# A linear-attention and maxout kernel: PSUM tiles of one bank, output in token order, loads given out sooner

## The chip, the cores and the metric

The kernel runs on one core of a Trainium2 chip. The core has a matrix engine (TensorE, PE in the profile), three engines for elementwise work (VectorE or DVE, ScalarE or ACT, GpSimd or POOL) and SyncE (SP), which gives out most transfers. Each engine runs its own instructions in program order and waits on semaphores for the others. Matrix products land in PSUM, a memory of eight banks of 2 KB for each of 128 partitions; everything else lies in SBUF. The metric is device time in microseconds, and less is better.

## The reference

The first part is a linear attention with a decaying state, for 4 batches and 8 heads, 768 tokens and a head dimension of 48. The second is a layer with two weight matrices, the elementwise maximum of both products, and an output matrix.

```python
for t in range(S):
    kt, vt, rt, wt = k[:, :, t], v[:, :, t], r[:, :, t], w[:, :, t]
    cur = np.einsum('bhd,bhe->bhde', u[None] * kt, vt)
    y[:, :, t] = np.einsum('bhd,bhde->bhe', rt, state + cur)
    state = wt[:, :, :, None] * state + np.einsum('bhd,bhe->bhde', kt, vt)
# ...
x = y.transpose(0, 2, 1, 3).reshape(B * S, H * D)      # 3072 x 384
g = np.maximum(x @ w1, x @ w2)                          # d_ff = 1024
out = g @ w_out                                         # 3072 x 384
```

## The kernel before

The tokens are cut into 12 units of 256 tokens of one batch (three chunks of time, four batches each). Within a unit a row of 128 partitions holds two neighbouring tokens each (index i, even and odd), and the lower and the upper 64 partitions are the two halves of the unit (index b). The maximum is computed as relu(x (w1 - w2)) + x w2, so wd is w1 - w2, and wc is w2 @ w_out, formed once at the start.

The kernel is written as small operations, one for each step and unit, and a string ORDER lists them. Every engine runs its operations in that order. A tile that comes from a pool with so many buffers may only be given out again when the last user of the old one is done; the waits follow from that. The names that matter, for a unit n:

- w, k, r, v: loads. lw: ScalarE takes the logarithm of w. lp: GpSimd adds the two tokens of a row. cs: TensorE makes running sums. m, z: VectorE puts the exponents together. AO, AE, iA: ScalarE exponentials. rp, kp: VectorE scales r and k with them. rk, rku, dg, vd: the token's own term (GpSimd, GpSimd, VectorE, GpSimd). vb: GpSimd casts v.
- tr: TensorE transposes the scaled r and k. ev0, ev1: ScalarE and VectorE copy the transposes to SBUF.
- kv, Sa, S1, Tf, dec, S0, row, WL, Wt: the state and its decay.
- sc0, sc1: scores of the even and the odd tokens. M0, M1: VectorE masks them. yb, yi, ya: the three parts of y, summed in PSUM. xT: ScalarE copies y to SBUF.
- g0 to g3, r0 to r3: gates (TensorE) and relu (ScalarE). oc, oa, ob: the output matrix in three parts, for each half b. os: ScalarE copies the output to SBUF. out: the store.
- wd, wt, wcm, wce: weights at the start.

A stretch of ORDER for the middle of the kernel, and the start of it:

```
w.0 lw.0 k.0 r.0 u w2 rk.0 rku.0 dg.0 lp.0 cs.0 m.0 z.0 AO.0 AE.0 rp.0 iA.0 kp.0 v.0 vb.0 w.1 w1
wd.0 k.1 r.1 lw.1 kv.0 Sa.0 Tf.0 S1.0 tr.0 ev0.0 ev1.0 wd.1 wo lp.1 cs.1 m.1 z.1 AO.1 AE.1 vd.0
...
M0.5 AO.6 AE.6 rp.6 g3.4 r3.4 oc0.4 oa0.4 sc1.5 M1.5 iA.6 kp.6 rk.6
rku.6 dg.6 v.6 w.7 lw.7 k.7 r.7 vb.6 ob0.4 oc1.4 oa1.4 os0.4 out0.4 row.5 WL.5 dec.3 S0.3 ya.5
xT.5 tr.6 ev0.6 ev1.6 ob1.4 os1.4 out1.4 g0.5 r0.5 kv.6 Sa.6 S1.6 Tf.6 Wt.4 lp.7 cs.7 m.7 z.7
g1.5 g2.5 r1.5 r2.5 vd.6 yb.6 yi.6 sc0.6 M0.6 AO.7 AE.7 rp.7 g3.5 r3.5 oc0.5 oa0.5 sc1.6 M1.6
```

The parts of the code that the change touches, with cuts:

```python
LB = 3
ldp = tc.alloc_tile_pool(name="ld", bufs=LB)             # loads
def load(n, name, src):
    U[n][name] = t = ldp.tile([P, H, 2, D], F32, tag="l" + name, name="l" + name)
    nc.sync.dma_start(out=..., in_=...)                   # 384 KB
# ...
def tr(n):                                                # "sc": one buffer of two banks
    U[n]["tr"] = tp = pt_([P, 2, 2, 2, NP, Q], BF16, "sc")
    # ... 32 transposes into tp[:, b, j, i, p, :]
def evict(n, b, copy):
    U[n]["T", b] = t = wt_([P, 2, 2, NP, Q], BF16, f"T{b}")
    copy(t..., U[n]["tr"][:, b]...)
# ...
def scores(n, i):
    U[n]["sc", i] = sc = pt_([P, 2, NP, P], F32, "sc")
    # ... 16 matmuls into sc[q, e, p, :]
def masked(n, i):
    U[n]["M", i] = t = wt_([P, 2, NP, P], BF16, f"M{i}")
    nc.vector.tensor_mul(t..., U[n]["sc", i]..., mask[:, i]...)   # 1024 elements
# ...
def xT(n):
    U[n]["xT"] = t = wt_([P, 2, KO, P], BF16, "xT", 3)
    nc.scalar.copy(t.rearrange("c b k t -> c b (k t)"), U[n]["y"][:, :, 0:HD])
def gate(n, j):                                           # "go": two buffers of one bank
    U[n]["g", j] = g = pt_([P, 2, 2, P], F32, "go", 2)
    # ... 6 matmuls
def out_s(n, b):                                          # five buffers
    U[n]["s", b] = t = wt_([P, HD], F32, "osb", 5)
    nc.scalar.copy(t, U[n]["o", b])
def out_d(n, b):
    for i in range(2):                                    # even tokens, odd tokens
        nc.sync.dma_start(out=out[tok + i:tok + P:2, :],
                          in_=U[n]["s", b][i * Q:(i + 1) * Q, :])
```

The eight PSUM banks: two for the sums (ex), two for y and kv (y), two for transposes and scores (sc), two for gates and outputs (go).

Of the kernel before, what the change touches and what calls it, by code (L numbers as in the profile page):

```python
# [22 lines left out]
wce.2 k.2 r.2 rp.2 v.2 w.3 lw.3 vb.2 k.3 r.3 ya.1 g3.0 oc0.0 oa0.0 r3.0 xT.1 iA.2 kp.2 rk.2
rku.2 dg.2 row.1 WL.1 ob0.0 oc1.0 oa1.0 os0.0 ob1.0 os1.0 out1.0 g0.1 r0.1 out0.0 kv.2 Sa.2 S1.2
Tf.2 tr.2 ev0.2 ev1.2 g1.1 g2.1 r1.1 r2.1 lp.3 cs.3 m.3 z.3 vd.2 yb.2 yi.2 sc0.2 M0.2 AO.3 AE.3
rp.3 g3.1 oc0.1 oa0.1 r3.1 sc1.2 M1.2 ob0.1 oc1.1 oa1.1 v.3 w.4 vb.3 lw.4 k.4 r.4 iA.3 kp.3
os0.1 out0.1 ya.2 xT.2 rk.3 rku.3 dg.3 row.2 WL.2 tr.3 ev0.3 ev1.3 Wt.1 ob1.1 os1.1 out1.1 g0.2
r0.2 kv.3 Sa.3 S1.3 Tf.3 lp.4 cs.4 m.4 z.4 g1.2 g2.2 r1.2 r2.2 dec.0 S0.0 vd.3 yb.3 yi.3 sc0.3
M0.3 AO.4 AE.4 rp.4 g3.2 r3.2 oc0.2 oa0.2 dec.1 S0.1 sc1.3 M1.3 iA.4 kp.4 v.4 w.5 k.5 r.5 lw.5
row.3 WL.3 ob0.2 oc1.2 oa1.2 os0.2 out0.2 ya.3 xT.3 rk.4 rku.4 dg.4 tr.4 ev0.4 ev1.4 ob1.2 os1.2  # L30
out1.2 g0.3 r0.3 vb.4 kv.4 Sa.4 S1.4 Tf.4 lp.5 cs.5 m.5 z.5 g1.3 r1.3 g2.3 r2.3 vd.4 yb.4 yi.4
sc0.4 M0.4 Wt.2 dec.2 S0.2 AO.5 AE.5 rp.5 g3.3 r3.3 oc0.3 oa0.3 sc1.4 M1.4 iA.5 kp.5 v.5 w.6 k.6
r.6 lw.6 vb.5 rk.5 rku.5 dg.5 ob0.3 oc1.3 oa1.3 os0.3 out0.3 ya.4 xT.4 Wt.3 row.4 WL.4 tr.5
ev0.5 ev1.5 ob1.3 os1.3 out1.3 g0.4 r0.4 kv.5 Sa.5 S1.5 Tf.5 lp.6 cs.6 m.6 z.6 g1.4 r1.4 g2.4
r2.4 vd.5 yb.5 yi.5 sc0.5 M0.5 AO.6 AE.6 rp.6 g3.4 r3.4 oc0.4 oa0.4 sc1.5 M1.5 iA.6 kp.6 rk.6
rku.6 dg.6 v.6 w.7 lw.7 k.7 r.7 vb.6 ob0.4 oc1.4 oa1.4 os0.4 out0.4 row.5 WL.5 dec.3 S0.3 ya.5
xT.5 tr.6 ev0.6 ev1.6 ob1.4 os1.4 out1.4 g0.5 r0.5 kv.6 Sa.6 S1.6 Tf.6 Wt.4 lp.7 cs.7 m.7 z.7
g1.5 g2.5 r1.5 r2.5 vd.6 yb.6 yi.6 sc0.6 M0.6 AO.7 AE.7 rp.7 g3.5 r3.5 oc0.5 oa0.5 sc1.6 M1.6
iA.7 kp.7 dec.4 S0.4 Wt.5 rk.7 rku.7 dg.7 v.7 vb.7 w.8 lw.8 k.8 r.8 row.6 WL.6 dec.5 S0.5 ob0.5
oc1.5 oa1.5 os0.5 out0.5 ya.6 xT.6 tr.7 ev0.7 ev1.7 ob1.5 os1.5 out1.5 g0.6 r0.6 kv.7 Sa.7 S1.7  # L40
Tf.7 lp.8 cs.8 m.8 z.8 g1.6 r1.6 g2.6 r2.6 vd.7 yb.7 yi.7 sc0.7 M0.7 AO.8 AE.8 rp.8 g3.6 r3.6
oc0.6 oa0.6 sc1.7 M1.7 iA.8 kp.8 v.8 w.9 vb.8 lw.9 k.9 r.9 rk.8 rku.8 dg.8 ob0.6 oc1.6 oa1.6
os0.6 out0.6 ya.7 xT.7 row.7 WL.7 tr.8 ev0.8 ev1.8 ob1.6 os1.6 out1.6 g0.7 r0.7 kv.8 Sa.8 S1.8
lp.9 cs.9 m.9 z.9 g1.7 g2.7 r1.7 r2.7 vd.8 yb.8 yi.8 sc0.8 M0.8 AO.9 AE.9 rp.9 g3.7 r3.7 oc0.7
oa0.7 sc1.8 M1.8 iA.9 kp.9 rk.9 rku.9 dg.9 v.9 w.10 k.10 r.10 lw.10 vb.9 Wt.6 dec.6 S0.6 ob0.7
oc1.7 oa1.7 os0.7 out0.7 ya.8 xT.8 tr.9 ev0.9 ev1.9 ob1.7 os1.7 out1.7 g0.8 r0.8 kv.9 Sa.9 S1.9
lp.10 cs.10 m.10 z.10 g1.8 r1.8 g2.8 r2.8 vd.9 yb.9 yi.9 sc0.9 M0.9 AO.10 AE.10 rp.10 g3.8 r3.8
oc0.8 oa0.8 sc1.9 M1.9 iA.10 kp.10 v.10 vb.10 w.11 lw.11 ob0.8 oc1.8 os0.8 out0.8 oa1.8 ya.9
xT.9 rk.10 rku.10 dg.10 tr.10 ev0.10 ev1.10 k.11 r.11 ob1.8 os1.8 out1.8 g0.9 r0.9 kv.10 Sa.10
S1.10 lp.11 cs.11 m.11 z.11 g1.9 r1.9 g2.9 r2.9 vd.10 yb.10 yi.10 sc0.10 M0.10 AO.11 AE.11 rp.11  # L50
g3.9 r3.9 oc0.9 oa0.9 sc1.10 M1.10 iA.11 kp.11 rk.11 rku.11 dg.11 v.11 vb.11 ob0.9 oc1.9 oa1.9
os0.9 out0.9 Wt.7 dec.7 S0.7 ya.10 xT.10 ob1.9 os1.9 out1.9 g0.10 r0.10 tr.11 ev0.11 ev1.11
kv.11 Sa.11 S1.11 g1.10 r1.10 g2.10 r2.10 vd.11 yb.11 yi.11 sc0.11 M0.11 g3.10 r3.10 oc0.10
oa0.10 sc1.11 M1.11 ob0.10 oc1.10 oa1.10 os0.10 out0.10 ya.11 xT.11 ob1.10 os1.10 out1.10 g0.11
r0.11 g1.11 r1.11 g2.11 r2.11 g3.11 r3.11 oc0.11 oa0.11 ob0.11 oc1.11 oa1.11 os0.11 out0.11
ob1.11 os1.11 out1.11
"""


# [19 lines left out]
def _body(tc, r, k, v, w, u_in, moe_w1, moe_w2, moe_w_out, out):  # L79
    nc = tc.nc  # L80
    B, H, S, D = r.shape
    P = 128
# [246 lines left out]

    def evict(n, b, copy):  # L330
        U[n]["T", b] = t = wt_([P, 2, 2, NP, Q], BF16, f"T{b}")
        copy(t.rearrange("d j i p q -> d (j i p q)"),  # L332
             U[n]["tr"][:, b].rearrange("d j i p q -> d (j i p q)"))
# [123 lines left out]
    @op  # L459
    def xT(n):  # L460
        U[n]["xT"] = t = wt_([P, 2, KO, P], BF16, "xT", 3)
        nc.scalar.copy(t.rearrange("c b k t -> c b (k t)"), U[n]["y"][:, :, 0:HD])  # L462
# [38 lines left out]
    def out_d(n, b):  # L501
        c, bb = unit(n)
        tok = bb * S + c * C + b * P
        for i in range(2):
            nc.sync.dma_start(out=out[tok + i:tok + P:2, :],  # L505
                              in_=U[n]["s", b][i * Q:(i + 1) * Q, :])
# [45 lines left out]
```

## Time and profile before

| | |
|---|---|
| time | 171.19 us, median of 3 (169.57 to 171.47) |
| span of the profiled execution | 170.9 us |
| TensorE matmul busy | 136.6 us, 80% of the span |
| VectorE, ScalarE, GpSimd busy | 98.6, 94.1 and 96.0 us |
| moved by DMA | 28.19 MB, 165 GB/s in the mean |
| loads of w, k, r, v | 12 each of 384 KB |
| stores | 48 of 96 KB |

A line of groups names the line of the kernel, the engine, the operation and the tiles, then how many, the busy time and the mean of one in ns, then the idle time of the engine just before and what ended it. A line of a timeline begins with the start and the duration in us; what ended the idle time before it stands in brackets. In the slices each digit is a fortieth of the span, in tenths of busy time. A line of waits names the engine that waited, what it waited for, and the total, the number and the longest of the waits. "SPq" is the time in which SyncE gives out a transfer. TensorE's matmuls are pipelined, so the duration of one holds more than its share of the engine.

### The profile page before, as it was taken

To read this page: it belongs to the slowest core of one execution; us is meant where nothing else is said; L and a number is where in the kernel's file an instruction comes from. 1 tells how busy PE (TensorE), PEld (TensorE's weight loads), DVE (VectorE), ACT (ScalarE), POOL (GpSimd) and SP (SyncE) were. 2 spreads that over 40 slices of the span, in tenths; PEclk is the share of its full clock that TensorE was granted. 3 is DMA by queue.
4 is the path that set the end of the run, shared out by engine and by line. 5 is a ranking of instruction groups with operands and counts; after the bars stand their busy time and mean duration, and the time that the engine had idled before them with its cause. 6 is when DMAs were issued, how large, how long until landed. Compare 5 with 4: busy or idle time off the path is not lost.

```text
span 170.9 us, 6596 instructions
## 1 busy us (share of the span) xinstructions
PE 136.6 (80%) x2920; PEld 90.0 (53%) x2920; DVE 98.6 (58%) x144; ACT 94.1 (55%) x165; POOL 96.0 (56%) x91
## 2 busy tenths in 40 slices
PE   0003273999999599999799995997989999989990
...
PEclk9999997599999879999999999999999999999999
...
GB/s 141 234 235 404 258 231 210 72 232 323 22 72 239 194 69 300 114 113 301 73 221 207 51 196 199 153 274 88 188 235 105 176 50 263 112 50 6 92 15 81
DMA packets 63182, 28.19 MB, mean 165 GB/s; under 512 B 58153, under 2 KB 62377, under 8 KB 63153
## 3 DMA queue, kind: packets, MB, share of 16 engines
...
q8 instruction: 23, 0.38, 0.9%
...
## 4 chain that ended last, share of the span: by engine, by line
PE 30%; DMA 26%; ACT 12%; POOL 9%; DVE 8%; SPq 7%; issue 5%; ACTq 0%; POOLq 0%; DVEq 0%
DMA lw<-in_w_dram 15%; PE go L470 8%; PE go L494 7%; DMA u_b<-in_u_dram 4%; SPq L505 4%; PE go L217 3%; PE go L489 3%; POOL rku L302 3%; ACT T L332 3%; SPq L179 3%; DMA lv<-in_v_dram 3%; ACT xT L462 3%; DMA lk<-in_k_dram 3%; PE ex L237 2%; POOL rku L297 2%
## 5 line engine op out<-in xcount | busy, mean ns | idle before, releaser
L470 PE MATMUL go<-xT,wd_sb 128*128 128x256 bf16 x288 | 37.9, 276 | 3.4 <-ACT xT L462 3.2
L494 PE MATMUL go<-wo_sb,gT 128*128 128x384 bf16 x192 | 39.2, 331 | 0.0
L397 DVE TENSOR_TENSOR M<-sc,mask 128x1024 bf16<-128x1024 f32 x24 | 29.4, 1223 | 13.7 <-PE sc L393 13.7
L470 PEld LDWEIGHTS <-wd_sb 128*128 128x128 bf16 x288 | 27.3, 99 | 13.1 <-issue 7.1
L478 ACT ACTIVATE gT<-go 128x512 bf16<-128x512 f32 x48 | 28.7, 601 | 9.9 <-PE go L470 8.3
L297 POOL TENSOR_TENSOR rku<-lr,lk 128x768 f32<-128x768 f32 x12 | 21.8, 1817 | 8.2 <-DMA lr<-in_r_dram 8.2
L292 POOL CAST vn<-lv 128x768 bf16<-128x768 f32 x12 | 9.9, 826 | 26.9 <-DMA lv<-in_v_dram 20.1
L237 PE MATMUL ex<-lp,triS 128*128 128x384 f32 x24 | 12.3, 599 | 14.2 <-POOL lp L233 14.2
L302 POOL TENSOR_TENSOR rku<-rku,u_b 128x768 f32<-128x768 f32 x12 | 21.8, 1814 | 3.1 <-DMA u_b<-in_u_dram 2.3
L494 PEld LDWEIGHTS <-gT 128*128 128x128 bf16 x192 | 17.3, 98 | 11.5 <-issue 0.3
L313 POOL TENSOR_TENSOR vd<-lv,dg 128x768 bf16<-128x768 f32 x12 | 19.6, 1633 | 4.5 <-DVE dg L308 4.3
L308 DVE TENSOR_REDUCE dg<-rku 128x16 f32<-128x768 f32 x12 | 11.4, 949 | 16.8 <-POOL rku L302 16.8
L228 ACT ACTIVATE lw<-lw 128x768 f32<-128x768 f32 x12 | 10.1, 840 | 15.2 <-DMA lw<-in_w_dram 15.2
L332 DVE COPY T<-sc 128x1024 bf16<-128x1024 bf16 x12 | 8.3, 689 | 13.4 <-ACT T L332 13.3
L489 PE MATMUL go<-wc_sb,xT 128*128 128x384 bf16 x72 | 15.6, 326 | 0.0
L255 ACT ACTIVATE ex<-mz 128x384 f32<-128x384 f32 x12 | 5.9, 490 | 17.2 <-DVE mz L251 17.2
L233 POOL TENSOR_TENSOR lp<-lw 128x384 f32<-128x384 f32 x12 | 12.0, 998 | 6.0 <-ACT lw L228 5.9
L263 ACT ACTIVATE ex<-mz 128x768 f32<-128x768 f32 x12 | 9.8, 816 | 8.8 <-DVE rn L267 8.8
L499 ACT COPY osb<-go 128x384 f32<-128x384 f32 x24 | 11.5, 480 | 5.6 <-PE go L494 5.6
L271 DVE TENSOR_TENSOR kn<-lk,ex 128x768 bf16<-128x768 f32 x12 | 11.4, 946 | 5.3 <-ACT ex L263 5.3
L267 DVE TENSOR_TENSOR rn<-lr,ex 128x768 bf16<-128x768 f32 x12 | 11.4, 948 | 2.2 <-ACT ex L259 1.7
L332 ACT COPY T<-sc 128x1024 bf16<-128x1024 bf16 x12 | 12.2, 1017 | 0.7 <-PE sc L325 0.6
...
## 6 DMA issues: line engine op xcount, KB each, us to landing
...
out_dram<-osb SPq DMA_DIRECT2D x48, 96.0 KB, 2.3
...
```

What stands on the lines that cost most here:

```text
L233: nc.gpsimd.tensor_add(t, U[n]["lw"][:, :, 0, :], U[n]["lw"][:, :, 1, :])
L237: nc.tensor.matmul(EX[:, 0, 0:HD], triS, U[n]["lp"].rearrange("p h d -> p (h d)"))
L297: nc.gpsimd.tensor_mul(t, U[n]["r"], U[n]["k"])
L302: nc.gpsimd.tensor_mul(t, t, u_b.rearrange("p (h d) -> p h d", h=H).unsqueeze(1).to_broadcast([P, 2, H, D]))
L313: nc.gpsimd.tensor_mul(t.rearrange("p i h d -> p h i d"), U[n]["v"], U[n]["dg"].to_broadcast([P, H, 2, D]))
L332: copy(t.rearrange("d j i p q -> d (j i p q)"), U[n]["tr"][:, b].rearrange("d j i p q -> d (j i p q)"))
L397: nc.vector.tensor_mul(t.rearrange("s e p t -> s (e p) t"), U[n]["sc", i].rearrange("s e p t -> s (e p) t"), mask[:, i].rearrange("s i q - ...
L470: nc.tensor.matmul(g[:, f, :], wd_sb[:, ko, fo * P:(fo + 1) * P], U[n]["xT"][:, :, ko, :], start=(f == 0 and ko == 0), stop=(f == 1 and ko ...
L478: nc.scalar.activation(U[n]["gT"][:, 2 * j:2 * j + 2].rearrange("p f j t -> p (f j t)"), U[n]["g", j].rearrange("p f j t -> p (f j t)"), A ...
L489: nc.tensor.matmul(t, U[n]["xT"][:, b, ko, :], wc_sb[:, ko, :], start=(ko == 0), stop=False)
L494: nc.tensor.matmul(U[n]["o", b], U[n]["gT"][:, fo, b, :], wo_sb[:, fo, :], start=False, stop=(fo == FO - 1))
L499: nc.scalar.copy(t, U[n]["o", b])
```

## The change

Five things change together. The PSUM tiles for transposes and scores become two buffers of one bank each, in place of one buffer of two banks; a transpose tile is now one half b, a score tile one parity e of the heads, and the mask is applied in two instructions (Ma, Mb). xT writes the tokens in their order, so that an output half is 128 neighbouring tokens and one store writes it. The load buffers become four. And ORDER is written anew: loads stand further ahead of their use, the stores later, and TensorE works on the gates and outputs of one unit between the steps of the next, in another order than before.

The two banks are for letting TensorE refill one while the other is still read; the single store is for fewer issues on SyncE; the loads and buffers are for keeping the loads from standing behind the stores.

```diff
-w.0 lw.0 k.0 r.0 u w2 rk.0 rku.0 dg.0 lp.0 cs.0 m.0 z.0 AO.0 AE.0 rp.0 iA.0 kp.0 v.0 vb.0 w.1 w1
-wd.0 k.1 r.1 lw.1 kv.0 Sa.0 Tf.0 S1.0 tr.0 ev0.0 ev1.0 wd.1 wo lp.1 cs.1 m.1 z.1 AO.1 AE.1 vd.0
 ... (cut)
+w.0 k.0 r.0 u w2 rk.0 lw.0 lp.0 cs.0 m.0 z.0 rku.0 dg.0 AO.0 AE.0 rp.0 v.0 vb.0 w.1 w1 wd.2 k.1
+lw.1 r.1 iA.0 kp.0 tr.0 ev1.0 ev0.0 kv.0 Sa.0 S1.0 Tf.0 wd.0 lp.1 cs.1 m.1 z.1 row.0 wo vd.0
+yb.0 yi.0 sc1.0 M1a.0 M1b.0 AO.1 AE.1 rp.1 iA.1 rk.1 rku.1 v.1 vb.1 w.2 wt.0 lw.2 lp.2 sc0.0
+M0a.0 WL.0 wcm.0 dg.1 M0b.0 ya.0 xT.0 wd.1 wt.1 wcm.1 wt.2 vd.1 wce.0 kp.1 tr.1 cs.2 ev1.1 kv.1
 ... (cut)
+dg.5 vd.5 rk.6 rku.6 out1.0 g0.3 g1.3 r0.3 r1.3 g2.3 r2.3 g3.3 r3.3 rp.5 iA.5 row.4 WL.4 sc0.4
+oc0.3 oa0.3 ob0.3 os0.3 out0.3 v.6 w.7 vb.6 k.7 r.7 M0a.4 M0b.4 ya.4 xT.4 kp.5 tr.5 ev0.5 ev1.5
+cs.6 m.6 z.6 kv.5 Sa.5 S1.5 AO.6 AE.6 Tf.5 oc1.3 oa1.3 ob1.3 os1.3 out1.3 Wt.4 dec.4 S0.4 Wt.2
+dec.2 S0.2 yb.5 yi.5 sc1.5 M1a.5 M1b.5 g0.4 r0.4 g1.4 r1.4 g2.4 r2.4 g3.4 r3.4 row.5 WL.5 rp.6
+iA.6 sc0.5 out1.2 oc0.4 oa0.4 lw.7 lp.7 row.6 ob0.4 os0.4 oc1.4 Wt.3 WL.6 dec.3 S0.3 dg.6 vd.6
 ... (cut)
-    LB = 3
+    LB = 4
 ... (cut)
-        U[n]["tr"] = tp = pt_([P, 2, 2, 2, NP, Q], BF16, "sc")
+        U[n]["tr"] = tp = [pt_([P, 2, 2, NP, Q], BF16, "sc", 2) for b in range(2)]
-                            tp[:, b, j, i, p, :],
+                            tp[b][:, j, i, p, :],
-             U[n]["tr"][:, b].rearrange("d j i p q -> d (j i p q)"))
+             U[n]["tr"][b].rearrange("d j i p q -> d (j i p q)"))
 ... (cut)
-        U[n]["sc", i] = sc = pt_([P, 2, NP, P], F32, "sc")
+        U[n]["sc", i] = sc = [pt_([P, NP, P], F32, "sc", 2) for e in range(2)]
-                    nc.tensor.matmul(sc[q, e, p, :], t[d, 1, i, p, :], t[d, 0, :, p, :])
+                    nc.tensor.matmul(sc[e][q, p, :], t[d, 1, i, p, :], t[d, 0, :, p, :])
 ... (cut)
-    def masked(n, i):
-        U[n]["M", i] = t = wt_([P, 2, NP, P], BF16, f"M{i}")
+    def masked(n, i, e):
+        if e == 0:
+            U[n]["M", i] = wt_([P, 2, NP, P], BF16, f"M{i}")
         nc.vector.tensor_mul(
-            t.rearrange("s e p t -> s (e p) t"),
-            U[n]["sc", i].rearrange("s e p t -> s (e p) t"),
-            mask[:, i].rearrange("s i q -> s (i q)").unsqueeze(1).to_broadcast([P, H, P]))
+            U[n]["M", i][:, e], U[n]["sc", i][e],
+            mask[:, i].rearrange("s i q -> s (i q)").unsqueeze(1).to_broadcast([P, NP, P]))
 ... (cut)
-        nc.scalar.copy(t.rearrange("c b k t -> c b (k t)"), U[n]["y"][:, :, 0:HD])
+        nc.scalar.copy(t.rearrange("c b k (q i) -> c (b k) i q", i=2),
+                       U[n]["y"][:, :, 0:HD].rearrange("c b (k i q) -> c b k i q", k=KO, i=2))
 ... (cut)
-        for i in range(2):
-            nc.sync.dma_start(out=out[tok + i:tok + P:2, :],
-                              in_=U[n]["s", b][i * Q:(i + 1) * Q, :])
+        nc.sync.dma_start(out=out[tok:tok + P, :], in_=U[n]["s", b])
```

More of the change, by code (lines that the diff above doesn't have):

```diff
@@ L17 @@
 ORDER = """
-w.0 lw.0 k.0 r.0 u w2 rk.0 rku.0 dg.0 lp.0 cs.0 m.0 z.0 AO.0 AE.0 rp.0 iA.0 kp.0 v.0 vb.0 w.1 w1
-wd.0 k.1 r.1 lw.1 kv.0 Sa.0 Tf.0 S1.0 tr.0 ev0.0 ev1.0 wd.1 wo lp.1 cs.1 m.1 z.1 AO.1 AE.1 vd.0
-yb.0 yi.0 sc0.0 M0.0 sc1.0 rp.1 M1.0 iA.1 kp.1 rk.1 rku.1 dg.1 wd.2 ya.0 xT.0 tr.1 ev0.1 ev1.1
-v.1 vb.1 w.2 wt.0 wt.1 wcm.0 lw.2 wce.0 kv.1 Sa.1 S1.1 Tf.1 wcm.1 wce.1 g0.0 r0.0 vd.1 yb.1 yi.1
-sc0.1 M0.1 g1.0 g2.0 r1.0 r2.0 sc1.1 M1.1 row.0 WL.0 Wt.0 lp.2 cs.2 m.2 z.2 AO.2 AE.2 wt.2 wcm.2
@@ L23 @@
[L23 to L56, printed above, removed]
+w.0 k.0 r.0 u w2 rk.0 lw.0 lp.0 cs.0 m.0 z.0 rku.0 dg.0 AO.0 AE.0 rp.0 v.0 vb.0 w.1 w1 wd.2 k.1
+lw.1 r.1 iA.0 kp.0 tr.0 ev1.0 ev0.0 kv.0 Sa.0 S1.0 Tf.0 wd.0 lp.1 cs.1 m.1 z.1 row.0 wo vd.0
+yb.0 yi.0 sc1.0 M1a.0 M1b.0 AO.1 AE.1 rp.1 iA.1 rk.1 rku.1 v.1 vb.1 w.2 wt.0 lw.2 lp.2 sc0.0
@@ new lines @@
+M0a.0 WL.0 wcm.0 dg.1 M0b.0 ya.0 xT.0 wd.1 wt.1 wcm.1 wt.2 vd.1 wce.0 kp.1 tr.1 cs.2 ev1.1 kv.1
+m.2 ev0.1 Sa.1 Tf.1 S1.1 z.2 AO.2 AE.2 wce.1 wcm.2 wce.2 yb.1 yi.1 sc1.1 M1a.1 M1b.1 g0.0 r0.0
+g1.0 r1.0 g2.0 g3.0 r2.0 r3.0 k.2 r.2 rk.2 rku.2 rp.2 iA.2 dg.2 v.2 vb.2 vd.2 w.3 lw.3 lp.3 k.3
+r.3 rk.3 rku.3 v.3 w.4 k.4 r.4 vb.3 sc0.1 oc0.0 oa0.0 ob0.0 os0.0 oc1.0 out0.0 M0a.1 M0b.1 ya.1
+xT.1 Wt.0 dec.0 S0.0 kp.2 tr.2 ev1.2 cs.3 ev0.2 kv.2 Sa.2 S1.2 Tf.2 oa1.0 ob1.0 os1.0 row.1 m.3
+WL.1 z.3 AO.3 AE.3 yb.2 yi.2 sc1.2 M1a.2 M1b.2 g0.1 g1.1 r0.1 r1.1 g2.1 g3.1 r2.1 r3.1 row.2
@@ new lines @@
+WL.2 sc0.2 oc0.1 oa0.1 rp.3 iA.3 lw.4 lp.4 v.4 w.5 vb.4 k.5 r.5 v.5 w.6 k.6 r.6 ob0.1 oc1.1
+os0.1 out0.1 dg.3 vd.3 rk.4 rku.4 M0a.2 M0b.2 ya.2 xT.2 vb.5 kp.3 tr.3 ev1.3 ev0.3 cs.4 m.4 kv.3
+Sa.3 S1.3 Tf.3 Wt.1 dec.1 S0.1 oa1.1 ob1.1 os1.1 out1.1 z.4 AO.4 AE.4 yb.3 yi.3 sc1.3 g0.2 g1.2
+r0.2 r1.2 g2.2 r2.2 g3.2 r3.2 M1a.3 M1b.3 sc0.3 rp.4 iA.4 lw.5 lp.5 oc0.2 oa0.2 ob0.2 oc1.2
+os0.2 out0.2 dg.4 vd.4 rk.5 rku.5 lw.6 lp.6 M0a.3 M0b.3 ya.3 xT.3 kp.4 tr.4 ev1.4 ev0.4 cs.5
+kv.4 Sa.4 S1.4 Tf.4 row.3 WL.3 m.5 oa1.2 ob1.2 os1.2 z.5 AO.5 AE.5 yb.4 yi.4 sc1.4 M1a.4 M1b.4
@@ new lines @@
+dg.5 vd.5 rk.6 rku.6 out1.0 g0.3 g1.3 r0.3 r1.3 g2.3 r2.3 g3.3 r3.3 rp.5 iA.5 row.4 WL.4 sc0.4
[3 more added lines that the diff above has]
+iA.6 sc0.5 out1.2 oc0.4 oa0.4 lw.7 lp.7 row.6 ob0.4 os0.4 oc1.4 Wt.3 WL.6 dec.3 S0.3 dg.6 vd.6
+rk.7 rku.7 M0a.5 M0b.5 ya.5 xT.5 kp.6 tr.6 ev1.6 ev0.6 cs.7 m.7 kv.6 Sa.6 S1.6 Tf.6 oa1.4 ob1.4
@@ new lines @@
+os1.4 z.7 AO.7 AE.7 yb.6 yi.6 sc1.6 M1a.6 M1b.6 g0.5 g1.5 r0.5 r1.5 g2.5 r2.5 g3.5 r3.5 rp.7
+iA.7 dg.7 sc0.6 v.7 w.8 k.8 r.8 vb.7 lw.8 lp.8 vd.7 v.8 w.9 vb.8 rk.8 rku.8 oc0.5 oa0.5 ob0.5
+os0.5 oc1.5 out0.5 M0a.6 M0b.6 ya.6 xT.6 kp.7 tr.7 ev0.7 ev1.7 cs.8 m.8 kv.7 Sa.7 S1.7 Tf.7
+out0.4 Wt.6 dec.6 S0.6 oa1.5 ob1.5 os1.5 z.8 AO.8 AE.8 yb.7 yi.7 sc1.7 M1a.7 M1b.7 g0.6 g1.6
+r0.6 r1.6 g2.6 r2.6 g3.6 r3.6 rp.8 iA.8 out1.4 dg.8 vd.8 sc0.7 lw.9 lp.9 oc0.6 oa0.6 ob0.6 os0.6
+M0a.7 M0b.7 ya.7 xT.7 oc1.6 k.9 r.9 rk.9 rku.9 v.9 w.10 k.10 r.10 vb.9 lw.10 lp.10 kp.8 tr.8
@@ new lines @@
+ev1.8 ev0.8 cs.9 kv.8 Sa.8 S1.8 oa1.6 ob1.6 os1.6 row.7 WL.7 m.9 z.9 AO.9 AE.9 Wt.5 dec.5 S0.5
+out0.6 dg.9 vd.9 rk.10 rku.10 yb.8 yi.8 sc1.8 g0.7 g1.7 r0.7 r1.7 g2.7 r2.7 g3.7 r3.7 M1a.8
+M1b.8 sc0.8 rp.9 iA.9 oc0.7 oa0.7 ob0.7 os0.7 oc1.7 M0a.8 M0b.8 ya.8 xT.8 kp.9 tr.9 ev1.9 ev0.9
+cs.10 m.10 kv.9 Sa.9 S1.9 oa1.7 ob1.7 os1.7 yb.9 yi.9 sc1.9 z.10 AO.10 AE.10 g0.8 g1.8 r0.8 r1.8
+g2.8 r2.8 g3.8 r3.8 M1a.9 M1b.9 sc0.9 oc0.8 oa0.8 ob0.8 oc1.8 rp.10 iA.10 v.10 w.11 vb.10 lw.11
+lp.11 k.11 r.11 v.11 dg.10 vd.10 rk.11 rku.11 Wt.7 dec.7 S0.7 out1.5 os0.8 M0a.9 M0b.9 ya.9 xT.9
@@ new lines @@
+kp.10 tr.10 ev1.10 ev0.10 cs.11 m.11 kv.10 Sa.10 S1.10 z.11 AO.11 oa1.8 ob1.8 os1.8 yb.10 yi.10
+sc1.10 M1a.10 M1b.10 AE.11 dg.11 vd.11 g0.9 r0.9 g1.9 r1.9 g2.9 r2.9 g3.9 r3.9 rp.11 iA.11
+sc0.10 oc0.9 oa0.9 ob0.9 M0a.10 M0b.10 ya.10 xT.10 out1.7 kp.11 tr.11 ev0.11 ev1.11 out0.7 oc1.9
+vb.11 kv.11 Sa.11 S1.11 oa1.9 ob1.9 out0.8 yb.11 yi.11 sc1.11 M1a.11 M1b.11 out1.6 os0.9 os1.9
+out1.9 g0.10 r0.10 g1.10 r1.10 g2.10 r2.10 g3.10 r3.10 out0.9 sc0.11 oc0.10 oa0.10 ob0.10 os0.10
+oc1.10 out0.10 out1.8 M0a.11 M0b.11 ya.11 xT.11 oa1.10 ob1.10 os1.10 g0.11 r0.11 g1.11 r1.11
@@ L57 @@
+g2.11 r2.11 g3.11 r3.11 oc0.11 oa0.11 ob0.11 os0.11 out0.11 out1.10 oc1.11 oa1.11 ob1.11 os1.11
+out1.11
 """
```

3 lines of the change are left out of this document (2 added, 1 removed).

## The prediction

> **What bounds the kernel now.** I read the page's engine shares and slices first, to see which engine could set the end and where it stands idle.
>
> ```profile
> PE 136.6 (80%) x2920; PEld 90.0 (53%) x2920; DVE 98.6 (58%) x144; ACT 94.1 (55%) x165; POOL 96.0 (56%) x91
> PE   0003273999999599999799995997989999989990
> PEclk9999997599999879999999999999999999999999
> ```
>
> TensorE is full from slice 7 on, with notches; no other engine passes 60%. The kernel has three parts: a start of 35 us with little TensorE work, a middle in which TensorE is nearly the bound, and a tail. Busy TensorE time by stretch (the view of windows) gives the notches a size: in the nine stretches of 11 us from 46 to 145 us it is busy 10.47, 9.56, 11.00, 10.12, 11.00, 9.21, 9.98, 10.48 and 10.81 us, together 92.63 of 99. So 6.4 us are idle there. A unit without an idle gap takes about 10.5 us: the transposed output copy (xT) of two late units starts at 127.23 and 137.95, 10.7 us apart, less 0.19 us of waiting.
>
> Next the waits and the chain, to see what makes the notches. The first two lines are SyncE's own waits over the span and ScalarE's from 46 to 145 us (total, times, longest); the third is the page's chain by line.
>
> ```profile
> SPq L505 <- ACT osb L499: 36.9, 12, 6.6
> ACT lw L228 <- DMA lw<-in_w_dram: 13.1, 7, 3.0
> DMA lw<-in_w_dram 15%; PE go L470 8%; PE go L494 7%; DMA u_b<-in_u_dram 4%; SPq L505 4%; PE go L217 3%; PE go L489 3%; POOL rku L302 3%; ACT T L332 3%; SPq L179 3%; DMA lv<-in_v_dram 3%; ACT xT L462 3%; DMA lk<-in_k_dram 3%; PE ex L237 2%; POOL rku L297 2%
> ```
>
> SyncE stands 36.9 us at output stores whose data isn't ready, and the loads of the next unit stand behind them in the same queue. The timelines of SyncE, ScalarE and TensorE around 100 us show one instance.
>
> ```profile
> 96.16 2.14 SPq L505 DMA_DIRECT2D out_dram<-osb  x2
> 98.39 0.54 SPq L179 DMA_DIRECT2D lv<-in_v_dram  x1
> 98.98 0.67 SPq L179 DMA_DIRECT2D lw<-in_w_dram  x1
> 103.46 0.84 ACT L228 ACTIVATE lw<-lw 128x768 f32<-128x768 f32 x1 [3.04 <-DMA lw<-in_w_dram]
> 104.21 0.46 ACT L499 COPY osb<-go 128x384 f32<-128x384 f32 x1
> 104.57 0.80 ACT L462 CAST xT<-y 128x768 bf16<-128x768 f32 x1
> 105.42 0.81 PE L470 MATMUL go<-xT,wd_sb 128*128 128x256 bf16 x6 [1.79 <-ACT xT L462]
> ```
>
> The w load goes out at 98.98 behind two stores and lands at about 103.4. ScalarE runs in program order, so the logarithm holds it for 3.04 us. The y data for xT was complete at about 102.3 (the last y matmuls begin at 101.51 and take 0.79), but xT starts at 104.57, and the gate matmuls stand 1.79 us. The cause of the largest notches is thus the place of the loads in SyncE's order, not bandwidth: in the stretch 101 to 112 us the DMA share is 0.80, from 90 to 101 us 0.55.
>
> **What the Trainium skill says.** "DMA: Bandwidth & Descriptors", section "Rules for kernel authors": issue a transfer early and wait for it late, and its set-up hides. The lines above are the opposite case, with a landing time of 5.1 us in the median for w. "PSUM — Partial Sum Buffer", section "PSUM bank collisions raise a hardware error": engines are to be kept apart by bank, while different banks may be read at once. Here both evictions of a transpose read banks of their own, and still run one after the other because they are in one tile: VectorE's waits for ScalarE's 13.3 us in 7 waits. "Perfetto Trace Analysis", section "Optimizing Scalar/DVE Operations": VectorE pays some 125 ns an instruction on PSUM. The trace agrees: 417 ns for 256 elements, 553 for 384 and 1223 for 1024 fit 145 + 1.06 ns an element. "TensorE: Matmul & The Clock Gate", Part 1: an idle TensorE falls to half clock, after some 3.4 us. In this trace a wait of only 1.97 us at 58.44, among small matmuls, was enough: the granted clock from 58.5 to 62 us is 0.55.
>
> **The change, part by part.**
>
> *Loads sooner, four buffers.* In the new order most loads stand about one unit ahead of their use (w.7 before the scores of unit 4 are masked, lw.7 after those of unit 5), and stores with data long ready (out1.0, out1.2, out0.4 and others) are pushed back behind them. This removes the waits of lw. What it can give is all TensorE idle time of the middle, 6.4 us, and the throttled clock after the wait at 58.44: four wo_sb matmuls take 1.39 us of the chain there against 0.65 elsewhere, six gate matmuls 1.28 against 0.76, the transposes 0.61 against 0.40, together 1.5 us. From 145 to 160 us two waits, 0.38 and 0.24 us, add 0.6. Sum: -8.5 us if nothing takes their place.
>
> *A new order on TensorE.* Now the gates of unit n follow the transposes, kv, half an output, yb, yi and the first scores of unit n+1, some 4 us after xT, so xT no longer holds them. But all four gates stand in one row, on two PSUM tiles (go). The only place where the old kernel did so is its tail:
>
> ```profile
> 159.71 3.03 PE L470 MATMUL go<-xT,wd_sb 128*128 128x256 bf16 x24 [0.24 <-ACT xT L462]
> 160.62 1.19 ACT L478 ACTIVATE gT<-go 128x512 bf16<-128x512 f32 x2 [0.58 <-PE go L470]
> ```
>
> 24 matmuls at the middle's pace (12 in 1.31 us of chain) would be 2.62, and about 0.15 more until the last one ends; they take 3.03. The third gate waits for the first relu, about 0.25 us. In ten units that is +2.5 us.
>
> *One-bank tiles.* Masking comes in halves of 512 elements: 145 + 1.06 x 512 = 688 ns by the fit, two of them 1.38 us against 1.22. 24 pairs add 24 x 0.15 = 3.6 us to VectorE, 0.3 us a unit on some 8.0 (the sum of its groups a unit), against 10.5: not on the path. In exchange scores may enter a bank when its half is masked, and both evictions run together, so T is whole 0.7 us sooner. In the new order TensorE has cs, kv and eight output matmuls (0.84 + 0.4 + 1.3 us) between the transposes and the first use of T, which covers 1.02 us of eviction either way. I count 0 for the tiles alone; they are what lets the new order run.
>
> *Token order.* xT reads and writes as many elements; I keep 0.80 us. One store for two halves SyncE's issues of some 0.6 us. Only the last store shows: SyncE issues until 168.20 and the span ends at 170.9. One issue less is -0.5, a store of twice the size perhaps +0.1: -0.4 us.
>
> *The start.* Old order on GpSimd: rk.0, rku.0, lp.0. New: lp.0 before rku.0.
>
> ```profile
> 10.77 1.80 POOL L302 TENSOR_TENSOR rku<-rku,u_b 128x768 f32<-128x768 f32 x1 [2.25 <-DMA u_b<-in_u_dram]
> 12.54 1.00 POOL L233 TENSOR_TENSOR lp<-lw 128x384 f32<-128x384 f32 x1
> 19.33 0.95 DVE L271 TENSOR_TENSOR kn<-lk,ex 128x768 bf16<-128x768 f32 x1 [0.88 <-ACT ex L263]
> 20.21 2.02 DVE L205 TENSOR_TENSOR wd_sb<-w1f,w_sb 128x1024 bf16<-128x1024 f32 x1
> ```
>
> lp.0 can begin at 8.5 (rk.0 ends there) instead of 12.54, so cs.0 begins at 9.6 instead of 13.58, and rp.0, which now also follows dg.0 (13.5), ends at 14.5 instead of 18.4. But the new order puts wd.2 before kp.0 on VectorE, and wd.2 needs all of w1. The DMA rate by single microseconds stands at 315 to 430 GB/s from 12 to 18 us (the long rows of w1) and falls to 204 by 19: w1 lands at about 18.5. wd.2 then ends at about 19.7 (1.22 us if GpSimd leaves it alone), and kp.0 ends at about 20.7, 0.4 later than now. The 4 us are lost to that wait. Further on, with the old durations: tr.0, T and Sa.0 until 23; wd.0, m.1 and z.1 until 25.3; masks and rp.1 (r.1 lands at about 25.5) until 27.7; dg.1 until 29.8 and the last mask until 30.5; wcm.0 meanwhile waits for the transposed w2 (some 29 us) and ends at 31.7; ya.0 until 32.4. That is 1.8 us later than now (ya.0 ends at 30.6), but with wcm.0 done, whose 2.67 us the old kernel still has ahead: a gain of 0.9, of which I count half, -0.5 us, as so many steps hang on it.
>
> *Sum.* -8.5 + 2.5 - 0.4 - 0.5 = -6.9. For waits that I can't name in an order so new, 0.15 us in each of 11 units, +1.7. Total -5.2 us: 171.2 - 5.2 = 166.0 us.
>
> **The rivals.** (a) Everything hides: the gates' wait is absorbed and no new one comes. Then 171.2 - 8.5 - 0.9 = 161.8 us. For it: VectorE, ScalarE and GpSimd have some 8 of 10.5 us a unit. Against: four gates in a row did wait in the tail. (b) The start decides: w1 lands late, wd.2 holds VectorE and with it kp.0, masks and all that follows. If each of w1, r.1 and the transposed w2 costs another microsecond, 169 us. For it: DMA share is 0.94 to 1.28 in the stretches up to 30 us. Against: most of the loads there keep their order. (c) In-order engines now wait for other things: dg and vd stand between the masks, and the stores pushed back hold their osb buffers, so an os may wait for a store behind five loads. Two such waits of 1 us every second unit would eat the whole gain: 171 us. Against: five osb buffers, and the late stores' data is ready long before. (d) The early loads were hidden anyway. Against it stand the 3.04 and 1.79 us above.
>
> **Range and chances.** From (a) to half of (c) gives 162 to 170. Faster by over 2% means under 167.8: my sum leaves 1.8 us for error, which I give 0.75. Within 2% 0.19, slower 0.06, as the latter needs waits larger than all those removed.
>
> **What would show it.** Right: lw's wait for its load under 4 us in the middle; xT no longer ahead of gate waits; TensorE idle under 4 us from 46 us to the last y; per unit one wait of gates for a relu of about 0.25 us; masks of about 690 ns; kp.0 at about 20 us behind a wd_sb that waited for w1; the two evictions of T side by side; xT at 0.80 us. Wrong: kp.0 at 16 to 17 us (then the start gives 3 us more), a throttled clock in the middle, xT much slower in its new layout, or osb copies that wait for stores.

## The result and the profile after

The kernel after takes 165.64 us in the median (165.07 to 166.10) beside 170.94 us for the kernel before: ratio 0.970, 95% interval 0.963 to 0.977. The prediction was 166.0 us, with a range of 162 to 170. The profiled spans are 163.9 and 170.9 us. They differ by 7.0 us where the medians differ by 5.3, because the execution of before that was profiled took 172.66 us; the steps below are compared in spans.

The page of the kernel after, engine shares, slices and chain:

```profile
PE 136.5 (83%) x2920; PEld 88.9 (54%) x2920; DVE 101.3 (62%) x168; ACT 98.6 (60%) x165; POOL 94.8 (58%) x91
PE   0041083599999999999999999999999999999991
PEclk9999999999999999999999999999999999999999
PE 79%; DMA 9%; SPq 4%; POOL 2%; ACT 1%; DVE 1%; issue 1%; ACTq 0%; DVEq 0%; POOLq 0%
```

From slice 8 on TensorE has no notch and its clock never falls below nine tenths; the chain that ended last is 79% TensorE, where it was 30% TensorE and 26% DMA before. In the window of 46 to 145 us TensorE is idle for 0.43 us (6.4 before), and the waits of lw for its load, 13.1 us before, are gone from the list. SyncE's largest wait stayed and even grew (36.9 us before), but lw no longer waits for a load that stands behind it:

```profile
SPq L508 <- ACT osb L503: 52.0, 10, 13.5
```

Two rows of groups answer to the prediction's steps for masks and xT (mean of one in ns after the comma):

```profile
L400 DVE TENSOR_TENSOR M<-sc,mask 128x512 bf16<-128x512 f32 x48 | 31.0, 685 | 14.5 <-PE sc L395 14.5
L465 ACT CAST xT<-y 128x768 bf16<-128x768 f32 x12 | 12.3, 1027 | 12.7 <-PE y L457 12.6
```

The half masks are at 685 ns as the fit said (688). xT is at 1027 ns, where the prediction kept 800.

The start, from the timelines of GpSimd and VectorE:

```profile
8.62 0.98 POOL L235 TENSOR_TENSOR lp<-lw 128x384 f32<-128x384 f32 x1
10.57 1.81 POOL L304 TENSOR_TENSOR rku<-rku,u_b 128x768 f32<-128x768 f32 x1 [0.96 <-DMA u_b<-in_u_dram]
18.56 1.45 DVE L207 TENSOR_TENSOR wd_sb<-w1f,w_sb 128x1024 bf16<-128x1024 f32 x1 [4.03 <-DMA w1f<-in_moe_w_dram]
19.93 0.94 DVE L273 TENSOR_TENSOR kn<-lk,ex 128x768 bf16<-128x768 f32 x1
```

lp runs 4 us sooner, and VectorE then stands 4.03 us for w1, so kp begins 0.6 us later than before.

Two points in the TensorE timeline split the 7.0 us into a start, a middle and a tail: the end of the last y matmuls of unit 1 and of unit 11. First before, then after:

```profile
41.53 0.79 PE L454 MATMUL y<-M,vn 64*32 64x128 bf16 x60
157.92 0.79 PE L454 MATMUL y<-M,vn 64*32 64x128 bf16 x64
```

```profile
46.04 0.79 PE L457 MATMUL y<-M,vn 64*32 64x128 bf16 x60
151.29 0.79 PE L457 MATMUL y<-M,vn 64*32 64x128 bf16 x64
```

The last y matmul of unit 1 ends at 42.32 us before and at 46.83 after; by then the new order has done g3, oc0, oa0, ob0 and oc1 of unit 0 in addition, 0.67 + 0.49 + 0.65 + 0.65 + 0.49 = 2.95 us, so the start costs 4.51 - 2.95 = +1.56 us. From there to the last y of unit 11 it is 116.39 us before and 105.25 after. In this stretch the new order has the 2.95 us less to do, and leaves 0.65 more for the tail (oa1 of unit 10), so the middle gains 11.14 - 3.60 = 7.54 us. The tail is 12.2 and 11.8 us, and with the 0.65 it gains 1.0. Sum: +1.6 - 7.5 - 1.0, about -7.0.

### The profile page after: what moved, and what is told of

It reads as the page before. It is cut to its first block, busy times and chain, and to the rows that moved or that the text cites. A ratio compares the mean times of both kernels' runs of the same rounds, so it can differ in the third digit from the quotient of the medians.

```text
span 163.9 us, 6574 instructions
## 1 busy us (share of the span) xinstructions
PE 136.5 (83%) x2920; PEld 88.9 (54%) x2920; DVE 101.3 (62%) x168; ACT 98.6 (60%) x165; POOL 94.8 (58%) x91
## 4 chain that ended last, share of the span: by engine, by line
PE 79%; DMA 9%; SPq 4%; POOL 2%; ACT 1%; DVE 1%; issue 1%; ACTq 0%; DVEq 0%; POOLq 0%
PE go L474 21%; PE go L498 20%; PE go L493 8%; DMA w2T_sb<-w_sb 6%; PE ex L239 6%; PE y L457 5%; PE sc L395 5%; PE sc L327 4%; PE go L219 4%; PE y L436 3%; DMA lr<-in_r_dram 3%; PE y L349 3%; SPq L279 2%; PE y L418 2%; SPq L181 1%; POOL rku L299 1%
## 5 line engine op out<-in xcount | busy, mean ns | idle before, releaser
L400 DVE TENSOR_TENSOR M<-sc,mask 128x512 bf16<-128x512 f32 x48 | 31.0, 685 | 14.5 <-PE sc L395 14.5
L474 PE MATMUL go<-xT,wd_sb 128*128 128x256 bf16 x288 | 35.5, 272 | 0.6 <-ACT gT L482 0.3
L498 PE MATMUL go<-wo_sb,gT 128*128 128x384 bf16 x192 | 35.2, 327 | 0.0
L498 PEld LDWEIGHTS <-gT 128*128 128x128 bf16 x192 | 18.0, 98 | 11.6
L315 POOL TENSOR_TENSOR vd<-lv,dg 128x768 bf16<-128x768 f32 x12 | 18.7, 1559 | 5.8 <-PE sc L395 3.4
L465 ACT CAST xT<-y 128x768 bf16<-128x768 f32 x12 | 12.3, 1027 | 12.7 <-PE y L457 12.6
L334 ACT COPY T<-sc 128x1024 bf16<-128x1024 bf16 x12 | 12.2, 1015 | 7.0 <-PE sc L327 7.0
L257 ACT ACTIVATE ex<-mz 128x384 f32<-128x384 f32 x12 | 6.0, 496 | 11.8 <-DVE mz L253 11.7
L395 PE MATMUL sc<-T 48*64 48x128 bf16 x384 | 10.7, 229 | 2.5 <-DVE M L400 2.5
```

The lines of the kernel that those rows point to most:

```text
L315: nc.gpsimd.tensor_mul(t.rearrange("p i h d -> p h i d"), U[n]["v"], U[n]["dg"].to_broadcast([P, H, 2, D]))
L334: copy(t.rearrange("d j i p q -> d (j i p q)"), U[n]["tr"][b].rearrange("d j i p q -> d (j i p q)"))
L395: nc.tensor.matmul(sc[e][q, p, :], t[d, 1, i, p, :], t[d, 0, :, p, :])
L400: nc.vector.tensor_mul(U[n]["M", i][:, e], U[n]["sc", i][e], mask[:, i].rearrange("s i q -> s (i q)").unsqueeze(1).to_broadcast([P, NP, P]))
L465: nc.scalar.copy(t.rearrange("c b k (q i) -> c (b k) i q", i=2), U[n]["y"][:, :, 0:HD].rearrange("c b (k i q) -> c b k i q", k=KO, i=2))
L474: nc.tensor.matmul(g[:, f, :], wd_sb[:, ko, fo * P:(fo + 1) * P], U[n]["xT"][:, :, ko, :], start=(f == 0 and ko == 0), stop=(f == 1 and ko ...
```

## The experiments

Theory A, that of the prediction: the loads stood behind stores in SyncE's queue, and the new place of the loads in ORDER removed that. Rival B: the new order on TensorE, with xT off the path, did it. Rival C: one of the parts counted as nearly nothing (tiles, token order, single store) did it. Ratios are to the kernel before on the same chip and leave out executions more than 1.5% above the fastest of their kernel, so they are not just the quotient of the two medians.

### Parts alone on the kernel before, and late loads in the kernel after

**b_early**: the loads from v.4, w.5, k.5 and r.5 on one unit sooner on SyncE, four buffers.

```diff
-LB = 3
+LB = 4
-... v.3 w.4 vb.3 lw.4 k.4 r.4 ... v.4 w.5 k.5 r.5 lw.5 ... v.5 w.6 k.6 r.6 lw.6 ...
+... v.3 w.4 vb.3 lw.4 k.4 r.4 v.4 w.5 k.5 r.5 ... v.5 w.6 k.6 r.6 lw.5 ... v.6 w.7 k.7 r.7 lw.6 ...
```

> The kernel before with its own order on every computing engine; only the loads from v.4, w.5, k.5 and r.5 on are given out one unit sooner, with four load buffers. If the place of the loads in SyncE's order made the idle time of the middle: 163.5 to 165.5 us, lw waits for its load under 3 us between 46 and 145 us, TensorE idle there under 2 us (6.4 before). If instead the new order on TensorE was needed: 169 to 171 us, the waits for xT stay.

Measured: 171.01 us (168.19 to 172.11) beside 171.76, ratio 0.989 (0.974 to 1.003). The interval holds both no change and a gain of 2.6%, and the median misses A's 163.5 to 165.5 us, so A in its plain form falls: lw waits only 2.3 us for its load in the profile, yet TensorE is idle 6.1 us from 46 to 145 us. B is not shown by this either, as the waits for xT, which it said would stay, are gone from TensorE's list. Another wait for SyncE stands in their place: z writes the buffer from which row is still to be read, and row stands behind the loads.

```profile
DVE mz L250 <- DMA row<-mz: 5.8, 4, 3.2
```

In the kernel before this wait is not in the list. One case can be followed: row goes out at 63.27 us behind eight loads and two stores, z starts at 65.57, and TensorE stands 1.43 us for the mask behind it. The other idle time of TensorE was not followed. The wait of the decayed state for Wt (8.1 us) tells less: it was 5.8 us before and is 7.2 us in b_swap below, which gains.

**b_tok**: token order and the single store, nothing else.

```diff
-        nc.scalar.copy(t.rearrange("c b k t -> c b (k t)"), U[n]["y"][:, :, 0:HD])
+        nc.scalar.copy(t.rearrange("c b k (q i) -> c (b k) i q", i=2),
+                       U[n]["y"][:, :, 0:HD].rearrange("c b (k i q) -> c b k i q", k=KO, i=2))
-        for i in range(2):
-            nc.sync.dma_start(out=out[tok + i:tok + P:2, :],
-                              in_=U[n]["s", b][i * Q:(i + 1) * Q, :])
+        nc.sync.dma_start(out=out[tok:tok + P, :], in_=U[n]["s", b])
```

> The kernel before with token order and one store for each half unit, nothing else. If only the last store counts: 170.3 to 170.9 us (0.4 less). If SyncE's issues were what held the loads back: 168 to 169 us, since a unit's stores take 1.2 us less. If the slower xT (1.03 us in place of 0.80) counts, since gates stand right behind it in this order: 171.5 to 173 us.

Measured: 164.32 us (163.32 to 164.68), ratio 0.958 (0.951 to 0.965). None of the three numbers held. This part alone gains at least as much as the whole change (0.970; the intervals just touch). Rival C is right for it, though the tie to the loads is that of theory A. SyncE's issues of stores (count, then shortest, median and longest in ns) first in the kernel before, then in b_tok, and ScalarE's wait in b_tok:

```profile
L505 SPq DMA_DIRECT2D out_dram<-osb x48: 466/587/1690, 47.2 to 167.6; - x48
```

```profile
L505 SPq DMA_DIRECT2D out_dram<-osb x24: 332/356/1577, 46.8 to 159.6; - x24
```

```profile
ACT lw L228 <- DMA lw<-in_w_dram: 4.4, 5, 1.3
```

By the medians a unit's stores take 4 x 0.587 = 2.35 us of SyncE before and 2 x 0.356 = 0.71 us in b_tok. Not all of that stands directly ahead of the loads, since in some units row and WL lie between the two halves. In SyncE's timelines the time from the first store directly ahead of a w load to giving out that load is 3.0 us before and 1.9 us in b_tok, in the mean over units 4 to 11. That is 1.1 us less, and lw's waits fell by as much: (13.1 - 4.4) / 8 = 1.1 us a unit.

**b_tiles**: tiles of one bank and halved masks, old order.

```diff
-        U[n]["tr"] = tp = pt_([P, 2, 2, 2, NP, Q], BF16, "sc")
+        U[n]["tr"] = tp = [pt_([P, 2, 2, NP, Q], BF16, "sc", 2) for b in range(2)]
-        U[n]["sc", i] = sc = pt_([P, 2, NP, P], F32, "sc")
+        U[n]["sc", i] = sc = [pt_([P, NP, P], F32, "sc", 2) for e in range(2)]
-... M0.n ... M1.n ...
+... M0a.n M0b.n ... M1a.n M1b.n ...
```

> The kernel before with tiles of one bank and the mask in halves, one behind the other, in the old order. If the tiles alone bring nothing: 170 to 172 us, masks of 685 ns, both evictions of T side by side. If sooner freed banks bring something by themselves: under 169 us.

Measured: 170.48 us (168.87 to 173.44), ratio 0.986 (0.977 to 0.995). The time is within the first expectation, with a gain of about 1%; lw still waits 11.7 us.

**a_late**: the kernel after with each load from unit 3 on directly ahead of its first use, and each store directly behind its copy.

```diff
-... os0.3 out0.3 v.6 w.7 vb.6 k.7 r.7 ... row.5 WL.5 ... out1.2 ... lw.7 ...
+... os0.3 out0.3 v.6 vb.6 ... row.5 WL.5 ... w.7 lw.7 ... k.7 r.7 rk.7 ...    (and each out directly behind its os)
```

> The kernel after, with SyncE's order as in the kernel before: each load from unit 3 on directly ahead of its first use, each store directly behind its copy; all other engines as after. If the place of the loads made the gain: 169 to 171 us, with lw waiting for its load 8 us or more between 46 and 145 us. If the TensorE order bears late loads: 165.5 to 167 us.

Measured: 194.31 us (190.87 to 195.07), against 171.76 for before. This is far outside both expectations. The edit is not SyncE's order of the kernel before: there w, k and r of the next unit are given out together, and k and r stand well ahead of rk, their first use. Here each load stands directly ahead of its first use, and GpSimd waits 16.0 us for r (3.3 before). So this run can't measure the share of the loads' place. In ScalarE's waits from 46 to 145 us:

```profile
ACT lw L228 <- DMA lw<-in_w_dram: 19.7, 6, 7.4
```

### What the kernel after needs of its parts

**a_same**: the kernel after, unchanged.

> The kernel after, unchanged, as the measure for the runs beside it on the same chip: 165.6 us.

Measured: 165.88 us (165.10 to 168.17), ratio 0.968 (0.961 to 0.974).

**a_lb3**: three load buffers in the kernel after.

```diff
-LB = 4
+LB = 3
```

> The kernel after with three load buffers. A load of the new order leads its use by about one unit, and the slot three units back is free by then: 165.6 us, within 0.5. If the fourth buffer is what lets loads go sooner: 168 us or more, with lw waiting for loads again.

Measured: 165.44 us (164.61 to 165.99), ratio 0.965 (0.958 to 0.972). The fourth buffer does nothing that can be measured.

**a_bank2**: tiles of two banks and whole masks in the new order.

```diff
-        U[n]["tr"] = tp = [pt_([P, 2, 2, NP, Q], BF16, "sc", 2) for b in range(2)]
+        U[n]["tr"] = tp = pt_([P, 2, 2, 2, NP, Q], BF16, "sc")
-        U[n]["sc", i] = sc = [pt_([P, NP, P], F32, "sc", 2) for e in range(2)]
+        U[n]["sc", i] = sc = pt_([P, 2, NP, P], F32, "sc")
-... M1a.n M1b.n ... M0a.n M0b.n ...
+... M1.n ... M0.n ...
```

> The kernel after with one tile of two banks for transposes and scores and the mask in one instruction, at the place of the second half. If the order covers evictions and masks either way: 165 to 166.5 us. If the split tiles are what lets the order run: 168 us or more, with TensorE waiting for masks or for T.

Measured: 168.00 us (167.47 to 168.58), ratio 0.982 (0.976 to 0.988), so 2.1 us more than a_same. TensorE is idle 2.1 us from 46 to 145 us (0.3 in a_same), and where an eviction on VectorE comes second it waits again for ScalarE's:

```profile
DVE T L331 <- ACT T L331: 5.7, 2, 3.1
```

The prediction counted 0 for the tiles alone and called them what lets the new order run.

**a_oldout**: the old layout of xT and two stores in the new order (the edit of b_tok backwards).

```diff
-        nc.sync.dma_start(out=out[tok:tok + P, :], in_=U[n]["s", b])
+        for i in range(2):
+            nc.sync.dma_start(out=out[tok + i:tok + P:2, :],
+                              in_=U[n]["s", b][i * Q:(i + 1) * Q, :])
```

> The kernel after with the old layout of xT and two stores for each half unit. xT back at 0.80 us; one issue more at the end: 165.9 to 166.2 us. If the 24 issues more delay loads: 167 us or more.

Measured: 167.95 us (167.67 to 169.13), ratio 0.983 (0.976 to 0.990), so 2.1 us more than a_same. In the middle little is lost (TensorE idle 0.4 us, lw waits 1.1 us), even with 48 stores. The last piece of SyncE's timeline, first in a_same, then in a_oldout:

```profile
144.62 16.02 SPq L508 DMA_DIRECT2D out_dram<-osb  x7
```

```profile
145.85 17.34 SPq L508 DMA_DIRECT2D out_dram<-osb  x14
```

In a_same SyncE is done at 160.64 us, 0.4 us after the last osb copy (160.28); in a_oldout at 163.19, 2.0 us after its own (161.23). Two stores each for out0.11, out1.10 and out1.11 queue up there. So with the loads out of the way the single store is worth 1.6 to 1.8 us at the end.

### What about the single store, where the loads stand, and the start

**b_tok2st**: token order, but two stores of 64 neighbouring tokens.

```diff
-        nc.sync.dma_start(out=out[tok:tok + P, :], in_=U[n]["s", b])
+        for i in range(2):
+            q = slice(i * Q, (i + 1) * Q)
+            nc.sync.dma_start(out=out[tok + i * Q:tok + (i + 1) * Q, :], in_=U[n]["s", b][q, :])
```

> The kernel before with xT in token order, as in b_tok, but each half unit stored in two pieces of 64 neighbouring tokens. If the number of issues on SyncE is what b_tok gains by (its single store takes 0.36 us to give out, the two of before 0.59 each): 169 to 171.5 us with issues of 0.5 us or more, 167 to 169 us if a piece of neighbouring rows goes out in 0.35 us. If instead whole stretches of output rows, or the layout of xT, are what counts: 164 to 165.5 us.

Measured: 171.72 us (169.88 to 174.28), ratio 1.005 (1.000 to 1.009). The gain is gone. It came from the number of stores, not from the layout. SyncE's issues, and ScalarE's wait from 46 to 145 us:

```profile
L507 SPq DMA_DIRECT2D out_dram<-osb x48: 466/587/1632, 46.4 to 167.3; - x48
```

```profile
ACT lw L228 <- DMA lw<-in_w_dram: 10.1, 6, 2.9
```

**b_swap**: in six units (from v.4 to v.9, with w, k and r of the next) the loads ahead of the second pair of stores; nothing else changed.

```diff
-... os1.4 out1.4 ... v.7 w.8 lw.8 k.8 r.8 ...
+... os1.4 v.7 w.8 k.8 r.8 out1.4 ... lw.8 ...
```

> The kernel before with one exchange in SyncE's order for each unit: the four loads of the group stand ahead of the unit's second pair of stores instead of behind it; three load buffers, all else as before. If stores ahead of the loads make the idle time: 165 to 168 us, lw waits for loads under 6 us from 46 to 145 us. If the gain of b_tok comes in another way than by sooner loads: 170 us or more.

Measured: 166.07 us (164.87 to 166.44), ratio 0.973 (0.966 to 0.981). This shows the mechanism by itself: 48 stores, old tiles, old TensorE order, three buffers, and still a gain of 4.6 us.

```profile
ACT lw L227 <- DMA lw<-in_w_dram: 3.8, 3, 2.4
```

**b_toktiles**: the edits of b_tok and b_tiles together.

> b_tok with tiles of one bank and masks in halves, in the old order. b_tok ran at 0.958 of before, the tiles alone at 0.986. If both gains add: 0.945, some 162.5 us. If the tiles helped only by covering late loads: 0.958, some 164.5 us.

Measured: 163.01 us (162.60 to 164.46), ratio 0.959 (0.952 to 0.966). In ratio this is no more than b_tok, as the second expectation had it. It is the fastest median of all runs, with the old order and three buffers. Its interval overlaps that of the kernel after only from 0.963 to 0.966.

**a_start**: the kernel after with the start in another order.

```diff
-... w1 wd.2 k.1 lw.1 r.1 iA.0 kp.0 ... Tf.0 wd.0 ... w.2 wt.0 lw.2 lp.2 sc0.0 M0a.0 WL.0 wcm.0 dg.1 M0b.0 ya.0 xT.0 wd.1 ...
+... w1 k.1 lw.1 r.1 iA.0 kp.0 ... Tf.0 ... w.2 wt.0 sc0.0 M0a.0 WL.0 M0b.0 ya.0 xT.0 kp.1 tr.1 dg.1 ... kv.1 wd.0 lw.2 lp.2
+    Sa.1 Tf.1 S1.1 wd.1 yb.1 yi.1 sc1.1 cs.2 m.2 z.2 AO.2 AE.2 wd.2 M1a.1 M1b.1 wcm.0 wce.0 wcm.1 wce.1 g0.0 ...
```

> The kernel after with the start in another order, up to the gates of unit 0: the three wd operations behind kp.0 and the first masks, lw.2 behind the evictions of unit 1, wcm behind ya.0 and the first scores of unit 1. If VectorE's wait for w1 and TensorE's for the transposed w2 are what the start of after loses: kp.0 at about 16.2 us, xT.0 before 28 us, 162 to 163.5 us in all. If the loads of r.1, v.1 and w.2 bound the start in any order: 165 to 166 us.

Measured: 166.32 us (165.76 to 167.37), ratio 0.977 (0.969 to 0.984). kp.0 begins at 17.04 us and xT.0 at 26.47 (34.35 in the kernel after), and still nothing is gained: the time is just above the second expectation, and the last y matmul of unit 1 ends at 47.45 us (46.83 in the kernel after). TensorE waits for the cast of v.1, whose load had not landed, and the window of 25 to 35 us has the clock at 0.50 (the columns after the engines' busy times are clock, DMA share and GB/s):

```profile
30.01 0.64 PE L347 MATMUL y<-vn,kn 64*64 64x64 bf16 x32 [2.63 <-POOL vn L292]
```

```profile
25.00:35.00 10.00, 5.93 (x167) 4.14 (x164) 6.74 (x9) 3.21 (x4) 4.45 (x4) 0.50 1.17 166
```

The runs side by side, with lw's waits for its load and TensorE's idle time, both from 46 to 145 us:

| | us | ratio | lw waits, us | TensorE idle, us |
|---|---|---|---|---|
| before | 170.94 | 1 | 13.1 | 6.4 |
| b_tok2st | 171.72 | 1.005 | 10.1 | 4.9 |
| b_early | 171.01 | 0.989 | 2.3 | 6.1 |
| b_tiles | 170.48 | 0.986 | 11.7 | 5.7 |
| b_swap | 166.07 | 0.973 | 3.8 | 2.7 |
| b_tok | 164.32 | 0.958 | 4.4 | 1.7 |
| b_toktiles | 163.01 | 0.959 | 3.3 | 1.2 |
| after | 165.64 | 0.970 | 0 | 0.4 |

The times come from several chips, so the ratios are to be compared. The two points used above for the kernel after place what is left between it and b_toktiles; in b_toktiles they are:

```profile
40.45 0.79 PE L456 MATMUL y<-M,vn 64*32 64x128 bf16 x60
148.73 0.80 PE L456 MATMUL y<-M,vn 64*32 64x128 bf16 x64
```

The middle is 108.3 us there, which is 8.1 us less than before; in b_tok it is 7.2 less, in b_swap 6.0, and in the kernel after 7.5 with its different share of work allowed for. So in these profiles the rewritten order gains nothing in the middle over the old order with fewer stores. Its start costs 46.83 - 2.95 - 41.24 = 2.64 us against b_toktiles.

## Why the prediction was right, and where its steps were not

**The bound and its cause held.** Loads behind stores in SyncE's queue held ScalarE at lw, and through xT (3.0 us of TensorE's waits from 46 to 145 us) and kp (2.0 us) TensorE. b_swap shows it with one exchange in SyncE's order. b_early points to its limit: the queue holds not only loads and stores, and loads given out further ahead delay row.

**Step "loads sooner", -8.5 us.** Measured, the middle gained 7.5 us net in spans, near the idle and throttled time that was counted; of the +2.5 and +1.7 us that the sum set against it there was little. But which part does it was wrong. "Token order ... Only the last store shows ... -0.4 us" is the step that failed: it counted only the last issue, and 36 of the 48 stores stand ahead of a load. At the end, too, it is more than 0.4 us: 1.6 to 1.8 us in the new order (a_oldout), since three halves queue there. Measured alone, that part gains 4.2% (b_tok), at least as much as the whole change. Loads sooner and stores cheaper cure the same wait, so they don't add: in the new order the single store is worth 2.1 us (a_oldout), in the old one 7.

**Step "new order on TensorE", +2.5 us.** Of the mechanism little is left. From the timeline of the kernel after and, second, of the kernel before (its first gate of that unit, at 105.42, is among the prediction's lines):

```profile
93.00 2.98 PE L474 MATMUL go<-xT,wd_sb 128*128 128x256 bf16 x24
95.91 0.42 PE L395 MATMUL sc<-T 48*64 48x128 bf16 x16
```

```profile
106.17 0.45 PE L347 MATMUL y<-vn,kn 64*64 64x64 bf16 x32
107.29 1.47 PE L470 MATMUL go<-xT,wd_sb 128*128 128x256 bf16 x12
108.70 0.35 PE L415 MATMUL y<-ident,vd 64*128 64x64 bf16 x12
109.57 0.83 PE L470 MATMUL go<-xT,wd_sb 128*128 128x256 bf16 x6
110.24 0.65 PE L489 MATMUL go<-wc_sb,xT 128*128 128x384 bf16 x3
```

Start to start the four gates take 2.91 us after, and 0.75 + 1.41 + 0.67 = 2.83 us before. The pace of 2.62 taken from the chain left out the steps between groups that the old order had too. The extra is 0.08 us a unit, 0.8 us over ten, not 2.5; both figures hold within 0.03 us in all units from 71 us on.

**Step "one-bank tiles", 0.** The duration was right (685 ns), and both evictions do run side by side. What they let the new order do is worth 2.1 us (a_bank2); in the old order with single stores they add nothing in ratio (b_toktiles).

**Step "token order", xT at 0.80 us.** It takes 1.03 us; in the new order, as in b_tok, this costs nothing that can be seen.

**Step "the start", -0.5 us.** It costs +1.6 us in the kernel after. wd.2 waited for w1 until 18.56 us, as predicted (18.5), and kp.0 ended at 20.9 (20.7). The slip came later: the transposed w2 let wcm.0 begin at 30.33 us (29 predicted), the three wd took 1.45, 2.65 and 1.80 us in place of 1.22 (each beside an instruction of GpSimd; the 1.22 was for one left alone), and ya.0 ended at about 34.3 (32.4). In a_start a shorter chain for unit 0 did not help, as unit 1 then stood.

**Waits without a name, +1.7 us.** There were nearly none: 0.43 us.

So the total came out right in part by luck, because terms cancel: the start 2.1 us worse, the middle 3.2 us better (-7.5 for a net -4.3), the tail 0.6 better, and the profiled span of before 1.7 us above what its median suggests. That the sum fell on 166.0 is not proof of its terms.

What stays open: b_tok and b_toktiles lie about 1% under the kernel after. The profiles place the difference in the start of the new order, but no run put the old start before the new middle. How much the new place of the loads is worth inside the new order was not measured either, since a_late missed it.
